# Grouped-query attention on one core: the order in which the transposed Q leaves PSUM

## The chip, the cores and the metric

The kernel runs on one core of a Trainium2 chip. The metric is the device time of one execution in microseconds; the smaller the better. A core has five engines that run their own instruction streams and meet only at semaphores: TensorE (PE: matmuls and transposes into PSUM; PEld is its loading of weights), VectorE (DVE), ScalarE (ACT), GpSimd (POOL) and SyncE (SP, which here only issues the DMAs). Inputs and outputs lie in HBM; SBUF is the working memory of 128 partitions, and PSUM takes TensorE's results.

## What is computed

Softmax attention with 32 query heads that share 8 key/value heads, for 16 sequences, 16 queries each, against 2048 keys. All inputs are bf16.

```
B, Hq, Hkv, Sq, Sk, D = 16, 32, 8, 16, 2048, 128
k = jnp.repeat(k, rep, axis=1)            # rep = Hq // Hkv = 4
v = jnp.repeat(v, rep, axis=1)
scores = jnp.einsum("bhqd,bhkd->bhqk", q, k) * D ** -0.5
p = softmax(scores, axis=-1)
return jnp.einsum("bhqk,bhkd->bhqd", p, v)
```

For each pair of a sequence and a key/value head there are 4 x 16 = 64 rows of Q, a K of 2048 x 128 and a V of 2048 x 128 (512 KB each). There are 16 x 8 = 128 such groups.

## The kernel before

**Tiling.** Two groups make a pair p, so that the 2 x 64 rows of Q fill 128 partitions; there are 64 pairs. Eight pairs share a chunk c of Q (1024 rows, `QCH`, line 19); there are 8 chunks.

**One pair** goes through these steps, each named as in the code. `K` and `V`: loads of two groups, 512 KB each. `kx` (L244, DVE, one for each group): a transpose of K in blocks of 32 x 32 words, two bf16 to a word, into `KT`. `S` (L327, PE): 32 matmuls of contraction length 32 into `S_ps`; since kx leaves the 128 values of d split into four parts, Q has to come in four matching parts x. `mx` (L251, DVE): scales the scores, copies them to `Sneg` and takes the row's extreme. `ex` (L254, ACT): exp into `P` (bf16), with the row sum. `pt` (L337, PE, two halves h): 16 transposes of P into `PT_ps`. `pe` (L274, ACT or DVE, two halves): copies `PT_ps` to `PT` in SBUF. `pv` (L342, PE): 32 matmuls of PT with V into `O_ps`. `rc` (L259, DVE): 1 / row sum. `nm` (L263 on ACT, L265 on DVE): scales and copies the result to `Osb`. `ST`: store.

**One chunk of Q** is made ready by these, each once for x = 0..3. `Q` is one load of 256 KB into `Qn`, in which partition a holds the NI = 8 rows 8a to 8a + 7. `qr` (L249; POOL, for chunk 0 DVE and ACT) picks from `Qn` the elements of part x and repeats them four times into `Qr`. `qt` (L315, PE): eight 128 x 128 transposes, one for each i, of `Qr` into `QT_ps`, one PSUM tile of 128 x 1024 bf16 whose column 128 i + a belongs to Q's row 8 a + i. `qe` (L274, ACT): copies `QT_ps` into `QT`, where column 8 a + i belongs to row 8 a + i, so that each pair's rows lie side by side for S. So qe is a copy with a change of order. There are 32 of them, and one `QT_ps`: qt of part x + 1 waits until qe of part x has read it (line 56).

**Order.** A planner in the file (`build_schedule`, lines 97 to 148) lays out a fixed order for every engine from a table of prices (`_DUR`, lines 23 to 28) and the dependencies of `make_ops` (lines 41 to 88). The engines then run these lists in order, with semaphore waits where a dependency crosses engines. In the table `("act", "qe")` stands at 1.06 us and `("act", "pe")` at 1.03. In the steady part the order of PE is S(p+1), pt(p), pv(p); of DVE mx(p), two kx, rc; of ACT ex(p), nm(p-1), pe(p, 0), pe(p, 1). Around the start of a chunk the four qr, qt and qe of the next-to-come chunk's pairs are worked in. For chunk 5 (the others from chunk 3 on are alike, eight pairs apart) the lists read:

```
ACT: ex.32 nm.31 qe.5.0 pe.32.1 qe.5.1 nm.32 qe.5.2 ex.33 qe.5.3 pe.33.0 ex.34 nm.33 pe.34.0 ex.35 nm.35 ex.36
PE:  pt.31 pv.31 qt.5.0 S.33 pt.32 qt.5.1 pv.32 qt.5.2 S.34 qt.5.3 pt.33 S.35 pv.33 pt.34 pv.34 S.36 pt.35
DVE: mx.32 kx.67 kx.68 rc.32 kx.69 pe.32.0 mx.33 kx.70 mx.34 rc.33 kx.71 pe.33.1 kx.72 mx.35 pe.34.1 rc.34 kx.73 nm.34
     rc.35 kx.74 pe.35.0 pe.35.1 mx.36
```

Chunk 0's four qt and qe come ahead of S.0; chunk 1's are spread over pairs 1 to 4.

**Loads and stores** all go through SP's queue, in the order ST(t-6), K of pair t, at times a Q, V of pair t-2. K has 10 buffers, V 14, O 8, KT and PT 3 each, Sneg and P 2 each, QT and Qn 2 each. SP waits in order, so a store that waits for its nm holds back the loads behind it.

Of the kernel before, what the change touches and what calls it, by code (L numbers as in the profile page):

```python
# [150 lines left out]
def bass_standalone__gqa_softmax__sampling_kernel(  # L151
# [14 lines left out]
    qch = min(QCH, NROWS)  # L166
    assert NROWS % qch == 0 and qch % 128 == 0
    NI = qch // 128
# [10 lines left out]
    QT = [sb(f"QT{i}", [128, 4, qch], BF16) for i in range(2)]  # L179
# [14 lines left out]
    QT_ps = ps("QT_ps", [128, 1024], BF16)  # L194
# [25 lines left out]
    def make_waiter(eng, me):  # L220
        seen = {}

        def waits(op):
            need = {}
            for d in deps[op]:
                if me == "pe" and d in where and where[d][0] == "pe":
                    continue
                s, n = wait_point(d)
                key = s.name
                if n > max(seen.get(key, 0), need.get(key, (None, 0))[1]):  # L230
                    need[key] = (s, n)
            for key, (s, n) in need.items():
                seen[key] = n
                eng.wait_ge(s, n)

        return waits

    def elementwise(eng, me):
        waits = make_waiter(eng, me)
        for op in progs[me]:  # L240
            kind, p = op[0], op[1]
            waits(op)
            if kind == "kx":
                ins = eng.transpose(KT[(p // 2) % NKT][:, p % 2, :], Kn[p % NBK][:, :])  # L244
            elif kind == "qr":
                x = op[2]
                dst = Qr[:, x, :, :].rearrange("m i (a d) -> m i a d", a=4)
                src = bass.AP(Qn[p % 2], (x // 2) * 64 + x % 2, [[NI * 128, 128], [128, NI], [0, 4], [2, 32]])
                ins = eng.activation(dst, src, ACT.Copy) if me == "act" else eng.tensor_copy(dst, src)  # L249
            elif kind == "mx":  # L250
                ins = eng.tensor_scalar(Sneg[p % 2][:, :], S_ps[:, :], -scale, None,  # L251
                                        op0=ALU.mult, op1=ALU.min, accum_out=nbias[:, p:p + 1])
            elif kind == "ex":
                ins = eng.activation(  # L254
                    P[p % 2][:, :].rearrange("m (r a j) -> m a r j", a=4, j=32),
                    Sneg[p % 2][:, :].rearrange("m (a r j) -> m a r j", a=4, j=32), ACT.Exp,
                    bias=nbias[:, p:p + 1], scale=-1.0, accum_out=rowsum[:, p:p + 1])
            elif kind == "rc":
                ins = eng.reciprocal(rrec[:, p:p + 1], rowsum[:, p:p + 1])  # L259
            elif kind == "nm":  # L260
                dst, src, r = Osb[p % NBO][:, :], O_ps[:, 0:128], rrec[:, p:p + 1]
                if me == "act":
                    ins = eng.activation(dst, src, ACT.Copy, scale=r)  # L263
                else:
                    ins = eng.tensor_scalar(dst, src, r, None, op0=ALU.mult)  # L265
            else:
                if kind == "qe":
                    dst = QT[p % 2][:, op[2], :].rearrange("d (a i) -> d i a", i=NI)
                    src = QT_ps[:, 0:qch].rearrange("d (i a) -> d i a", i=NI)
                else:  # L270
                    h = op[2]
                    dst = PT[p % NPT][:, 8 * h:8 * (h + 1), :]
                    src = PT_ps[h][:, :].rearrange("k (t m) -> k t m", t=8)
                ins = eng.activation(dst, src, ACT.Copy) if me == "act" else eng.tensor_copy(dst, src)  # L274
            ins.then_inc(sem_eng[me], 1)

    with nc.Block() as block:  # L277

        @block.gpsimd
        def _(gp):  # L280
            gp.iota(iota_t[:, :], [[1, 128]], base=0, channel_multiplier=-1).then_inc(sem_id, 1)
            gp.wait_ge(sem_id, 1)
            gp.tensor_scalar(ident[:, :], iota_t[:, :], 0.0, None, op0=ALU.is_equal).then_inc(sem_id, 1)
            elementwise(gp, "pool")
# [65 lines left out]
        @block.vector  # L350
        def _(dve):
            elementwise(dve, "dve")

        @block.scalar
        def _(act):
            elementwise(act, "act")
# [28 lines left out]
```

## Time and profile before

| | |
|---|---|
| median of 3 runs | 478.08 us (477.15 to 480.02) |
| the profiled execution's own time | 474.86 us |
| its span, from the first to the last instruction | 473.1 us |
| PE busy | 275.6 us (58%) |
| mean granted clock of TensorE | 0.825 of full speed |
| bytes read from HBM / written | 136.31 MB / 2.10 MB |

The span in 40 slices of 11.8 us: each digit is the busy share of an engine in tenths (9 is 90% or more), PEclk the clock that was granted to TensorE in tenths, and the last line what the DMA engines moved.

```profile
PE   1147547737655566646666456654666645675754
PEld 1115435525443354433544234442544424454543
DVE  5237567936795478955799366993579645889994
ACT  6859987999499966999588993899948799479894
POOL 0200000300003000110003000030000300000000
PEclk9999877975898677966899667995579776779999
DMA  8951978995889549995599839998299972999990
GB/s 300 413 220 49 348 265 286 360 413 182 308 315 401 197 169 407 352 361 182 213 406 400 319 133 332 340 408 306 89 353 320 401 278 115 340 337 363 411 367 10
```

A digit 3 of POOL marks the four qr of a chunk, so the chunks can be counted from that line. In a list of groups, a row has the line, the engine and its operation, output and input by name and shape, the count, then busy time and mean duration in ns, then the engine's idle time ahead of such instructions and what ended it. Matmuls overlap in the array, so their durations don't add up to PE's time.

### The profile page before, as it was taken

Reading aid. Unit: us, or ns where it says so; the run is one execution under the profiler, and the core shown is the slowest. Engines: PE = TensorE matmul, PEld = TensorE weight load, DVE = VectorE, ACT = ScalarE, POOL = GpSimd, SP = SyncE. Lnnn points to the kernel's source line nnn. Section 1 sums busy time; section 2 is a strip of 40 time slices with the busy share of each in tenths; the row PEclk is TensorE's granted clock in tenths of the full one; section 3 lists DMA queues with packets and bytes.
Section 4 is the critical chain, followed back from the end, with each engine's and each line's share of the span. In section 5 each row is a group of like instructions: output and inputs, shape, how many; then the busy total and the mean of one; then the engine's idle time right before and its main releaser. Section 6 shows DMA issues by size and latency. Waiting matters only on the chain.

```text
span 473.1 us, 11999 instructions
## 1 busy us (share of the span) xinstructions
PE 275.6 (58%) x5376; PEld 194.3 (41%) x5376; DVE 327.2 (69%) x369; ACT 381.1 (81%) x308; POOL 28.9 (6%) x34
## 2 busy tenths in 40 slices
PE   1147547737655566646666456654666645675754
PEld 1115435525443354433544234442544424454543
DVE  5237567936795478955799366993579645889994
ACT  6859987999499966999588993899948799479894
POOL 0200000300003000110003000030000300000000
PEclk9999877975898677966899667995579776779999
DMA  8951978995889549995599839998299972999990
GB/s 300 413 220 49 348 265 286 360 413 182 308 315 401 197 169 407 352 361 182 213 406 400 319 133 332 340 408 306 89 353 320 401 278 115 340 337 363 411 367 10
DMA packets 47282, 139.19 MB, mean 294 GB/s; under 512 B 13440, under 2 KB 13440, under 8 KB 47232
## 3 DMA queue, kind: packets, MB, share of 16 engines
q1 hardware_dynamic: 47232, 138.43, 77.9%
q8 instruction: 42, 0.69, 0.6%
q14 instruction: 8, 0.07, 0.0%
HBM read 136.31 MB, written 2.10 MB: 293 GB/s over the span
## 4 chain that ended last, share of the span: by engine, by line
issue 16%; ACT 14%; PE 12%; DVE 4%; DMA 3%; POOL 1%; SPq 1%; ACTq 0%; POOLq 0%
ACT PT L274 7%; ACT QT L274 5%; PE S_ps L327 4%; PE O_ps L342 4%; PE PT_ps L337 3%; DMA Qn<-in_q_dram 3%; ACT P L254 2%; DVE Sneg L251 1%; DVE PT L274 1%; POOL Qr L249 1%; DVE KT L244 1%; PE QT_ps L315 1%; SPq L301 1%; ACTq L277 0%; ACT O L263 0%
## 5 line engine op out<-in xcount | busy, mean ns | idle before, releaser
L251 DVE TENSOR_SCALAR_CACHE_REDUCE Sneg<-S_ps 128x2048 f32<-128x2048 f32 x64 | 146.5, 2289 | 66.2 <-PE S_ps L327 64.1
L274 ACT ACTIVATE QT<-QT_ps 128x1024 bf16<-128x1024 bf16 x32 | 151.1, 4723 | 13.5 <-PE QT_ps L315 13.4
L244 DVE STREAM_TRANSPOSE KT<-Kn 128x1024 int32<-128x1024 int32 x128 | 153.5, 1225 | 2.4 <-DMA Kn<-in_k_dram 2.3
L254 ACT ACTIVATE P<-Sneg,nbias 128x2048 bf16<-128x2048 f32 x64 | 129.3, 2020 | 8.8 <-DVE Sneg L251 8.6
L342 PE MATMUL O_ps<-Vb,PT 128*64 128x128 bf16 x2048 | 82.6, 243 | 77.1 <-ACT PT L274 69.8
L274 ACT ACTIVATE PT<-PT_ps 128x1024 bf16<-128x1024 bf16 x92 | 94.9, 1072 | 31.2 <-PE PT_ps L337 31.2
L342 PEld LDWEIGHTS O_ps<-Vb,PT 128*64 128x64 bf16 x2048 | 71.2, 125 | 92.6 <-ACT PT L274 81.9
L327 PE MATMUL S_ps<-KT,QT 32*64 32x512 bf16 x2048 | 89.5, 469 | 21.3 <-DVE KT L244 13.7
L337 PE MATMUL PT_ps<-ident,P 128*128 128x128 bf16 x1024 | 84.4, 248 | 11.8 <-ACT P L254 11.6
L337 PEld LDWEIGHTS PT_ps<-ident,P 128*128 128x128 bf16 x1024 | 72.2, 113 | 40.5 <-ACT P L254 29.0
L315 PE MATMUL QT_ps<-ident,Qr 128*128 128x128 bf16 x256 | 27.0, 270 | 84.6 <-ACT QT L274 56.7
L315 PEld LDWEIGHTS QT_ps<-ident,Qr 128*128 128x128 bf16 x256 | 20.4, 120 | 93.0 <-issue 77.6
L327 PEld LDWEIGHTS S_ps<-KT,QT 32*64 32x64 bf16 x2048 | 30.7, 120 | 49.8 <-issue 20.7
L249 POOL COPY Qr<-Qn 128x1024 bf16<-128x1024 bf16 x28 | 28.0, 1040 | 347.9 <-DMA Qn<-in_q_dram 346.7
L274 DVE COPY PT<-PT_ps 128x1024 bf16<-128x1024 bf16 x36 | 24.1, 689 | 32.1 <-PE PT_ps L337 32.0
L263 ACT ACTIVATE O<-O_ps,rrec 128x128 bf16<-128x128 f32 x53 | 20.9, 394 | 30.6 <-PE O_ps L342 30.3
L259 DVE RECIPROCAL rrec<-rowsum 128x1 f32<-128x1 f32 x64 | 9.1, 143 | 24.7 <-ACT P L254 24.6
L265 DVE TENSOR_SCALAR O<-O_ps,rrec 128x128 bf16<-128x128 f32 x11 | 3.9, 351 | 14.8 <-PE O_ps L342 14.8
L254 ACT ACTIVATION_READ_ACCUMULATOR P<-Sneg,nbias 128x1 f32 x64 | 12.5, 195 | 0.0
L251 DVE DVE_READ_ACCUMULATOR Sneg<-S_ps 128x1 f32 x64 | 5.3, 83 | 0.0
L249 DVE COPY Qr<-Qn 128x1024 bf16<-128x1024 bf16 x2 | 1.3, 690 | 3.4 <-DMA Qn<-in_q_dram 3.4
L249 ACT ACTIVATE Qr<-Qn 128x1024 bf16<-128x1024 bf16 x2 | 2.0, 1050 | 1.4 <-DMA Qn<-in_q_dram 1.4
(7 smaller groups left out, 2.5 us busy)
## 6 DMA issues: line engine op xcount, KB each, us to landing
Kn<-in_k_dram SPq DMA_DIRECT2D x128, 512.0 KB, 6.4
Vb<-in_v_dram SPq DMA_DIRECT2D x128, 512.0 KB, 8.0
Qn<-in_q_dram SPq DMA_DIRECT2D x8, 256.0 KB, 6.1
out_dram<-O SPq DMA_DIRECT2D x64, 32.0 KB, 4.7
```

Source lines behind the costliest of these rows:

```text
L244: ins = eng.transpose(KT[(p // 2) % NKT][:, p % 2, :], Kn[p % NBK][:, :])
L249: ins = eng.activation(dst, src, ACT.Copy) if me == "act" else eng.tensor_copy(dst, src)
L251: ins = eng.tensor_scalar(Sneg[p % 2][:, :], S_ps[:, :], -scale, None, op0=ALU.mult, op1=ALU.min, accum_out=nbias[:, p:p + 1])
L254: ins = eng.activation(P[p % 2][:, :].rearrange("m (r a j) -> m a r j", a=4, j=32), Sneg[p % 2][:, :].rearrange("m (a r j) -> m a r j", a= ...
L259: ins = eng.reciprocal(rrec[:, p:p + 1], rowsum[:, p:p + 1])
L263: ins = eng.activation(dst, src, ACT.Copy, scale=r)
L274: ins = eng.activation(dst, src, ACT.Copy) if me == "act" else eng.tensor_copy(dst, src)
L301: sp.dma_start(dst, src).then_inc(sem_dma[kind][s], 16)
L315: ins = pe.transpose(QT_ps[:, 128 * i:128 * (i + 1)], Qr[:, x, i, :], ident[:, :],)
L327: ins = pe.matmul(S_ps[64 * gg:64 * (gg + 1), 512 * a:512 * (a + 1)], QT[c % 2][32 * a:32 * (a + 1), x, 128 * pp + 64 * gg:128 * pp + 64 * ...
L337: ins = pe.transpose(PT_ps[h][:, 128 * t:128 * (t + 1)], P[p % 2][:, 128 * r:128 * (r + 1)], ident[:, :])
L342: ins = pe.matmul(O_ps[64 * gg:64 * (gg + 1), 0:128], PT[p % NPT][:, r, 64 * gg:64 * (gg + 1)], Vb[(2 * p + gg) % NBV][:, r, :], start=(r ...
```

## The change

In qe the loop order of the copy is turned round. Before, the copy walks `QT_ps` in its own order (i outside, a inside), reads 1024 columns in one run, and writes each at column 8 a + i of `QT`: consecutive writes are 8 elements (16 bytes) apart. After, it walks `QT` in its own order (a outside, i inside), writes 1024 columns in one run, and reads column 128 i + a of `QT_ps`: consecutive reads are 128 elements (256 bytes) apart, eight of them for each a. Every element goes from the same place to the same place as before. Nothing else in the kernel is touched.

```
             else:
                 if kind == "qe":
-                    dst = QT[p % 2][:, op[2], :].rearrange("d (a i) -> d i a", i=NI)
-                    src = QT_ps[:, 0:qch].rearrange("d (i a) -> d i a", i=NI)
+                    dst = QT[p % 2][:, op[2], :].rearrange("d (a i) -> d a i", i=NI)
+                    src = QT_ps[:, 0:qch].rearrange("d (i a) -> d a i", i=NI)
                 else:
                     h = op[2]
```

## The prediction

> **What bounds the kernel now.** I read the page's shares first, then its groups, then the order of time around one hand-over to a new Q chunk, then waits, chain and windows. From the page:
>
> ```profile
> span 473.1 us, 11999 instructions
> ...
> PE 275.6 (58%) x5376; PEld 194.3 (41%) x5376; DVE 327.2 (69%) x369; ACT 381.1 (81%) x308; POOL 28.9 (6%) x34
> ...
> q1 hardware_dynamic: 47232, 138.43, 77.9%
> ...
> L274 ACT ACTIVATE QT<-QT_ps 128x1024 bf16<-128x1024 bf16 x32 | 151.1, 4723 | 13.5 <-PE QT_ps L315 13.4
> ...
> L254 ACT ACTIVATE P<-Sneg,nbias 128x2048 bf16<-128x2048 f32 x64 | 129.3, 2020 | 8.8 <-DVE Sneg L251 8.6
> L274 ACT ACTIVATE PT<-PT_ps 128x1024 bf16<-128x1024 bf16 x92 | 94.9, 1072 | 31.2 <-PE PT_ps L337 31.2
> ...
> L249 ACT ACTIVATE Qr<-Qn 128x1024 bf16<-128x1024 bf16 x2 | 2.0, 1050 | 1.4 <-DMA Qn<-in_q_dram 1.4
> ...
> out_dram<-O SPq DMA_DIRECT2D x64, 32.0 KB, 4.7
> ```
>
> ACT is the fullest engine, and its largest group is the one that the change touches. The two L274 rows are copies of the same size by the same engine from PSUM to SBUF: PT takes 1.07 us, QT 4.72 us. They differ in the order of the elements: QT's write steps 16 bytes between 2-byte elements. But 81% is a mean over two stages. The order of time around the start of one chunk (qe.5, pairs 32 to 36) parts them; the columns are start, duration, engine, line, operation, and in brackets the idle time before it:
>
> ```profile
> 239.13 2.29 DVE L251 TENSOR_SCALAR_CACHE_REDUCE Sneg<-S_ps 128x2048 f32<-128x2048 f32 x1
> ...
> 253.36 2.29 DVE L251 TENSOR_SCALAR_CACHE_REDUCE Sneg<-S_ps 128x2048 f32<-128x2048 f32 x1
> ...
> 255.58 2.37 DVE L244 STREAM_TRANSPOSE KT<-Kn 128x1024 int32<-128x1024 int32 x2
> 255.70 2.00 ACT L254 ACTIVATE P<-Sneg,nbias 128x2048 bf16<-128x2048 f32 x1
> ...
> 255.87 1.08 PE L342 MATMUL O_ps<-Vb,PT 128*64 128x128 bf16 x32 [1.58 <-ACT PT L274]
> ...
> 258.02 1.08 PE L327 MATMUL S_ps<-KT,QT 32*64 32x512 bf16 x32
> ...
> 258.12 4.76 ACT L274 ACTIVATE QT<-QT_ps 128x1024 bf16<-128x1024 bf16 x1
> ...
> 259.03 1.07 PE L337 MATMUL PT_ps<-ident,P 128*128 128x128 bf16 x16
> 259.69 0.69 DVE L274 COPY PT<-PT_ps 128x1024 bf16<-128x1024 bf16 x1 [0.55 <-PE PT_ps L337]
> ...
> 263.02 0.66 PE L315 MATMUL QT_ps<-ident,Qr 128*128 128x128 bf16 x8 [2.93 <-ACT QT L274]
> ...
> 263.83 1.92 PE L342 MATMUL O_ps<-Vb,PT 128*64 128x128 bf16 x32
> ...
> 269.52 1.93 PE L327 MATMUL S_ps<-KT,QT 32*64 32x512 bf16 x32
> ...
> 271.52 2.29 DVE L251 TENSOR_SCALAR_CACHE_REDUCE Sneg<-S_ps 128x2048 f32<-128x2048 f32 x1 [7.78 <-PE S_ps L327]
> ...
> 276.19 1.89 PE L337 MATMUL PT_ps<-ident,P 128*128 128x128 bf16 x16 [0.69 <-ACT P L254]
> ...
> 292.12 2.28 DVE L251 TENSOR_SCALAR_CACHE_REDUCE Sneg<-S_ps 128x2048 f32<-128x2048 f32 x1
> ```
>
> From mx.29 (239.13) to mx.32 (253.36) three pairs take 14.23 us, 4.74 a pair: the dense stage. From mx.32 to mx.36 (292.12) four pairs take 38.76 us, 9.7 a pair: the hand-over. PE executes in order: qt.5.1 (263.02) waits for QT_ps, which ACT is still emptying, S.34 (269.52) stands behind qt.5.2, and DVE idles 7.78 us for S.34. The wait list says it for the whole span (total us, times, longest):
>
> ```profile
> DVE Sneg L251 <- PE S_ps L327: 64.1, 14, 15.6
> PE QT_ps L315 <- ACT QT L274: 56.7, 18, 4.9
> ```
>
> The chain that ended last shows mx.36 and mx.52, two chunks of eight pairs later: 116.9 us, so 58.5 a chunk.
>
> ```profile
> 292.21 2.21 DVE Sneg L251 x2
> ...
> 409.11 2.21 DVE Sneg L251 x2
> ```
>
> What binds the dense stage, and what DMA can do, the windows show (stretch, busy us of PE, PEld, DVE, ACT, POOL, then granted clock, DMA share, GB/s):
>
> ```profile
> 8.00:28.00 20.00, 3.06 (x24) 2.33 (x24) 6.23 (x5) 16.45 (x4) 4.04 (x4) 1.00 1.03 412
> ...
> 232.00:263.00 31.00, 18.04 (x448) 12.76 (x433) 30.05 (x34) 24.04 (x25) 3.99 (x4) 1.00 1.03 404
> ...
> 430.00:460.00 30.00, 19.51 (x495) 14.17 (x492) 29.64 (x31) 26.47 (x32) 0.00 (x0) 1.00 1.01 398
> ```
>
> In the dense windows DVE is busy 30.05 of 31.00 us and the DMA engines are full at about 400 GB/s. So the hand-over is bound by ACT's QT copies, the dense stage by DVE, with DMA at its heels.
>
> **The change, part by part.** It removes and adds no instruction, wait, semaphore or DMA. The planner's prices are untouched, so every engine's order (SP's queue too) stays; line 27 prices qe at 1.06 us, so the order is one laid out for a copy of that length. Only the 32 QT copies change: the write becomes one run of 2048 bytes, and the read takes 128 runs of eight elements that lie 256 bytes apart in PSUM.
>
> Price of the new copy. No row of the trace reads PSUM at a step. Low end: 1.05 us, the Qr row, where ACT reads SBUF at a 4-byte step and pays nothing for it. High end: 4.72 us, if jumps in a read cost what they cost in a write; more than that is not excluded (rival 3). I take 1.07 us: after the edit the copy has the PT row's engine, size, types, memories and write, and differs from it in the order of the read alone. The P row, whose write hops between 64-byte runs at 0.99 ns an element, shows that a jump now and then is not dear.
>
> [...]
>
> At 1.07 us each copy is 3.65 us shorter, in all 32 x 3.65 = 116.8 us of ACT. What of it lies on the path:
>
> (a) Start. The first QT copy starts at 5.64, the sixth transpose of K ends at 14.56, and S.0 starts at 28.11:
>
> ```profile
> 5.64 4.70 ACT L274 ACTIVATE QT<-QT_ps 128x1024 bf16<-128x1024 bf16 x1 [0.24 <-PE QT_ps L315]
> ...
> 8.21 6.35 DVE L244 STREAM_TRANSPOSE KT<-Kn 128x1024 int32<-128x1024 int32 x5 [1.96 <-DMA Kn<-in_k_dram]
> ```
>
> ```profile
> 28.11 1.93 PE L327 MATMUL S_ps<-KT,QT 32*64 32x512 bf16 x32 [4.88 <-ACT QT L274]
> ```
>
> Between stand only four transposes and four copies by turns, so S.0 starts 4 x 3.65 = 14.6 us sooner, at 13.5, and ends at 15.4, when DVE is free (14.56). Nothing of this is covered.
>
> (b) Six hand-overs, qe.2 to qe.7. Walked with the durations above, from the first mx at 0: ex 2.3 to 4.3, then nm, qe.0 to 5.8, ACT's PT copy (pt ends 6.7) to 7.8, qe.1 to 8.9, nm, qe.2 9.6 to 10.7, ex of the second pair to 12.8, qe.3 to 13.9, PT copy to 15.0, ex of the third pair to 17.1. On PE, qt.2 runs right behind pv at 9.0, and S of the third pair starts at 9.6. On DVE the third mx starts at 10.8, the fourth at 16.3 behind two kx and a PT copy, the fifth at 23.8 behind two kx, an nm and three PT copies. So 23.8 us for four pairs instead of 38.8: 15.0 saved, six times, 90 us. DVE is busy for some 22 of the 23.8; what is late next is DVE itself and no longer S.
>
> (c) The hand-over of chunk 1, spread over pairs 1 to 4, has the same four copies: 14.6 us on ACT. DVE would still need some 6 us a pair, so I count 12.
>
> Sum: 14.6 + 90 + 12 = 117, all of ACT's gain; 473.1 - 117 = 356. From the other side, DVE's work is 327.2 us; with 7 idle before mx.0, some 2 us of stall in each of seven hand-overs, and 10 at the end, 358.
>
> Then the cover: SP issues loads behind stores that wait for nm, so earlier nm means earlier loads, and DMA becomes the other bound. The first windows show the slow start:
>
> ```profile
> 0.00:5.00 5.00, 0.40 (x5) 0.43 (x6) 1.29 (x2) 2.89 (x3) 0.97 (x6) 1.00 0.59 190
> 5.00:10.00 5.00, 0.61 (x6) 0.34 (x4) 3.03 (x3) 4.76 (x2) 0.00 (x0) 1.00 0.95 369
> ...
> 270.00:275.00 5.00, 1.97 (x38) 0.88 (x23) 2.30 (x2) 5.00 (x2) 0.00 (x0) 0.50 0.98 348
> ```
>
> 138.43 MB at 412 to 398 GB/s take 336 to 348 us; the first ten us move 2.8 MB, which is 3 us lost; and K.127 lands six V loads (3.1 MB, 7.8 us) before V.127, while it has kx, S, mx, ex, pt, two PT copies, pv, nm and a store (4.7) ahead, some 15 us with waits, so the end lies 6 to 9 us behind the last V. Together 345 to 360. A chunk thus needs 17.3 MB / 0.400 = 43.3 us of DMA and 23.8 + 4 x 4.74 = 42.8 of DVE and ACT. Two bounds of one height will wait for each other at times: I add 4 to 358, a choice that no row measures. Span 362.
>
> The profiled execution took 474.86 us, 1.8 over its span, and the median of the runs is 478.08, 3.2 more. 362 + 1.8 + 3.2 = **367 us**.
>
> **The rivals.**
>
> 1. The read pays what the write paid. For it: the only row with a large step is dear. Against it: that row is a write of half-words, and no row shows a slow read. The copy stays at 4.7 us and the time at 478, within 0.5%. [...] Chance 0.05.
> 2. The read goes at half pace: 2 x 0.99 ns x 1024 = 2.0 us, 0.95 over the forecast, DVE's slack taking a tenth: 367 + 32 x 0.95 x 0.9 = 394 us. For and against as in 1. Chance 0.08.
> 3. Slower: PSUM's read is dearer than SBUF's write. Its place is the same copy; it decides from 4.72 us up, and each further us costs 32, since (a) to (c) put all of it on the path: at 6 us, 478 + 41 = 519. For it: 256 bytes is a longer step than 16. Against it: ACT's other groups read PSUM (PT) or hop (P, Qr), and none but the stepped write is slow. Chance 0.04.
> 4. The copy is short, but TensorE's granted clock stays low in the hand-overs. The window at 270 was granted 0.50, and there S takes 1.93 us against 1.08, pt 1.89 against 1.07, pv 1.92 against 1.08: 2.5 us more a pair, about half of it on the path. In 28 hand-over pairs that is 35 us, 402 at worst, and 385 if half of them are cold. Against it: the dense window at 232 was granted 1.00 with PE idle 13 of 31 us, and the stretch at 270 comes behind waits of PE for ACT (2.93 us at 263.02), which go. Chance 0.07.
>
> That the edit doesn't do what it says can be left out: both forms bring element (i, a) of QT_ps to place 8a + i of QT.
>
> **How the numbers follow.** Forecast 0.76; rivals 0.05, 0.08, 0.04 and 0.07. The forecast's own range is 354 (nothing lost where the bounds meet, DMA at 412) to 382 (DMA at 398 and 15 us lost there). With the half-cold case it reaches to 388; left out are rivals 1 to 3 and the worst of 4, 0.2 together. So 354 to 388. Faster by over 0.5% (about what a measurement of this kernel can tell from no change): 0.76 + 0.08 + 0.07 = 0.91; within 0.5%: 0.05; slower: 0.04.
>
> **What the new profile would show.** The QT row of L274 near 1.07 us, ACT busy near 265 us; S.0 near 13.5; hand-overs near 24 us for four pairs, without a wait of DVE for S_ps over 2 us in them; DMA share over 0.95 in nearly all of the span, and DVE busy for about 90% of it. The prediction is wrong at its first step if the QT row is over 1.3 us. It is wrong in its sum if the row is short but DVE still waits long for S (order or clock), or if waits of L244 for Kn pass some 15 us (DMA under 398 GB/s).

## The result, and the profile after

The changed kernel took 373.31 us (median of 4 runs, 367.76 to 375.11) against 478.79 us before (477.15 to 480.02): 0.772 of the time, 95% interval 0.764 to 0.781. Two of the four runs (374.96 and 375.11) count as slow, being over 1.5% above the fastest, and the ratios here and below compare fast runs alone. The forecast was 367 us, the range 354 to 388. In two later comparisons the same kernel gave 371.88 and 369.66 us; the 12 runs together lie between 366.75 and 376.26, median 371.6. The profiled execution took 371.66 us, with a span of 369.9.

The page of the changed kernel: shares, slices, the queue, and the groups that answer to those shown of before.

```profile
span 369.9 us, 11999 instructions
## 1 busy us (share of the span) xinstructions
PE 250.0 (68%) x5376; PEld 177.2 (48%) x5376; DVE 325.7 (88%) x369; ACT 268.0 (72%) x308; POOL 28.9 (8%) x34
...
DVE  4889899999749888999698999979989989799993
ACT  5387778966649477894587957869388865788883
...
PEclk9999699997878869998598998989879987899999
DMA  7999999999999799999999999999999999999960
GB/s 266 416 408 410 410 409 410 410 411 411 411 411 348 264 413 361 395 415 404 400 360 402 400 375 381 382 414 385 379 406 361 409 362 408 400 376 411 410 241 9
...
q1 hardware_dynamic: 47232, 138.43, 96.1%
...
L274 ACT ACTIVATE PT<-PT_ps 128x1024 bf16<-128x1024 bf16 x92 | 90.2, 1021 | 46.0 <-PE PT_ps L337 46.0
...
L274 ACT ACTIVATE QT<-QT_ps 128x1024 bf16<-128x1024 bf16 x32 | 32.6, 1020 | 9.8 <-PE QT_ps L315 9.8
```

The QT row fell from 4723 to 1020 ns and is now the PT row to a nanosecond: ACT's read of PSUM at a 256-byte step costs nothing here. ACT lost 113 us of work (381.1 to 268.0); PE's and DVE's instructions are the same. DVE has become the fullest engine at 88%, and the DMA engines are busy for 96% of the span instead of 78%, at 410 GB/s in long stretches. Two things in the slices are not as they should be: at slices 13 and 14 (about 110 to 130 us) the rate drops to 348 and 264 GB/s, and the granted clock still has digits of 5 and 6.

The wait list after (total us, times, longest):

```profile
PE O_ps L342 <- ACT PT L274: 57.6, 40, 1.6
...
DVE Sneg L251 <- PE S_ps L327: 16.6, 18, 1.7
...
PE QT_ps L315 <- POOL Qr L249: 5.3, 4, 3.2
...
PE QT_ps L315 <- ACT QT L274: 3.8, 4, 1.2
```

DVE's wait for S fell from 64.1 to 16.6 us, its longest from 15.6 to 1.7; PE's wait for the QT copies from 56.7 to 3.8. PE's wait for qr, that is for Q's load, was there before with 4.5 us in four waits, the longest 2.2; now its longest is 3.2.

### The profile page after: what moved, and what is told of

Same layout as the page of the kernel before. It is cut to its first block, busy times and chain, and to the rows that moved or that the text cites. A ratio compares the mean times of both kernels' runs of the same rounds, so it can differ in the third digit from the quotient of the medians.

```text
span 369.9 us, 11999 instructions
## 1 busy us (share of the span) xinstructions
PE 250.0 (68%) x5376; PEld 177.2 (48%) x5376; DVE 325.7 (88%) x369; ACT 268.0 (72%) x308; POOL 28.9 (8%) x34
## 3 DMA queue, kind: packets, MB, share of 16 engines
q1 hardware_dynamic: 47232, 138.43, 96.1%
## 5 line engine op out<-in xcount | busy, mean ns | idle before, releaser
L251 DVE TENSOR_SCALAR_CACHE_REDUCE Sneg<-S_ps 128x2048 f32<-128x2048 f32 x64 | 146.3, 2287 | 18.5 <-PE S_ps L327 16.6
L342 PE MATMUL O_ps<-Vb,PT 128*64 128x128 bf16 x2048 | 76.0, 232 | 71.9 <-ACT PT L274 57.6
L274 ACT ACTIVATE PT<-PT_ps 128x1024 bf16<-128x1024 bf16 x92 | 90.2, 1021 | 46.0 <-PE PT_ps L337 46.0
L342 PEld LDWEIGHTS O_ps<-Vb,PT 128*64 128x64 bf16 x2048 | 65.4, 117 | 86.0 <-ACT PT L274 65.3
L327 PE MATMUL S_ps<-KT,QT 32*64 32x512 bf16 x2048 | 83.1, 437 | 22.9 <-DVE KT L244 18.7
L337 PEld LDWEIGHTS PT_ps<-ident,P 128*128 128x128 bf16 x1024 | 65.4, 106 | 36.4 <-ACT P L254 25.1
L337 PE MATMUL PT_ps<-ident,P 128*128 128x128 bf16 x1024 | 77.2, 235 | 7.9 <-ACT P L254 7.5
L327 PEld LDWEIGHTS S_ps<-KT,QT 32*64 32x64 bf16 x2048 | 29.4, 113 | 48.1 <-DVE KT L244 24.5
L274 ACT ACTIVATE QT<-QT_ps 128x1024 bf16<-128x1024 bf16 x32 | 32.6, 1020 | 9.8 <-PE QT_ps L315 9.8
L263 ACT ACTIVATE O<-O_ps,rrec 128x128 bf16<-128x128 f32 x53 | 19.3, 364 | 28.2 <-PE O_ps L342 27.9
L274 DVE COPY PT<-PT_ps 128x1024 bf16<-128x1024 bf16 x36 | 23.8, 680 | 11.6 <-PE PT_ps L337 11.3
L315 PE MATMUL QT_ps<-ident,Qr 128*128 128x128 bf16 x256 | 22.7, 240 | 14.5 <-POOL Qr L249 5.3
L315 PEld LDWEIGHTS QT_ps<-ident,Qr 128*128 128x128 bf16 x256 | 17.3, 107 | 19.3 <-issue 8.4
L251 DVE DVE_READ_ACCUMULATOR Sneg<-S_ps 128x1 f32 x64 | 5.3, 83 | 0.0
```

What stands on the lines that cost most here:

```text
L315: ins = pe.transpose(QT_ps[:, 128 * i:128 * (i + 1)], Qr[:, x, i, :], ident[:, :],)
L327: ins = pe.matmul(S_ps[64 * gg:64 * (gg + 1), 512 * a:512 * (a + 1)], QT[c % 2][32 * a:32 * (a + 1), x, 128 * pp + 64 * gg:128 * pp + 64 * ...
L337: ins = pe.transpose(PT_ps[h][:, 128 * t:128 * (t + 1)], P[p % 2][:, 128 * r:128 * (r + 1)], ident[:, :])
L342: ins = pe.matmul(O_ps[64 * gg:64 * (gg + 1), 0:128], PT[p % NPT][:, r, 64 * gg:64 * (gg + 1)], Vb[(2 * p + gg) % NBV][:, r, :], start=(r ...
```

## The experiments

**Where the time of a chunk lies.** The 64 `mx` rows (DVE, L251) in order of time give the pace; mx.8c to mx.8c+4 is a hand-over of four pairs, mx.8c+4 to mx.8c+8 the four dense pairs behind it. Means over chunks 3 to 7 (the pairs 16 to 55), worked out from these starts in each profile; `clock` is the mean granted clock of TensorE in the five stretches of dense pairs, the last column the median time of the runs (for the changed kernel's first row that of all its 12):

```
kernel                           hand-over   dense   clock   chunk   span    median
before                              38.6      19.6    0.93    58.2   473.1   478.8
the prediction's walk               23.8      19.0            42.8
changed                             24.7      20.8    0.84    45.4   369.9   371.6
changed, the two later profiles     25.9      20.7    0.85    46.7   374.4   371.9
                                    24.5      20.9    0.84    45.4   369.8   369.7
changed, QT copies made twice       26.0      20.7    0.85    46.7   381.9   383.3
changed, every other copy slow      33.4      18.8    1.00    52.3   428.0   428.0
changed, Q's loads a pair earlier   22.5      21.9    0.77    44.5   361.5   362.8
changed, transposes added           25.7      19.4    0.93    45.1   366.1   367.1
changed, both of these              22.8      19.8    0.91    42.6   356.6   358.2
changed, half of V loaded           22.8      21.1    0.83    43.9   362.5   365.3
```

So the walk of the hand-over was 0.9 us short and the dense pairs 1.8: together 2.6 us a chunk and 13 us in these five chunks, about the 12 that separate the span from the walk's 358. Of the 1.8 us, 0.6 were there before the change: the walk took its 4.74 us a pair from a stretch with a granted clock of 1.00, and the five stretches before have 19.6 us for four pairs. In all rows the dense pairs are the slower the lower their clock, from 18.8 us at 1.00 to 21.9 at 0.77. Three profiles of the one changed kernel differ by 1.4 us in the hand-over and by 0.2 in the dense pairs, so a difference of 1 us in a hand-over shows little.

**1. The price of the copy by its step.** Behind the last pair, copies of one 128 x 1024 tile are made one at a time, each on its own line, with the step of the read or the write varied:

```
+            act.activation(y2(b_, 8), y1(q_, 8), ACT.Copy) ...      # read PSUM at 256 bytes
...
+            act.activation(x1(b_, 2), x2(q_, 2), ACT.Copy) ...      # write bf16 at 4 bytes
...
```

> After the last pair, copies of one 128 x 1024 tile are made one at a time into tiles that nobody reads, each on a line of its own, with the step of the read or the write varied; the answer is the duration of each. [...]

From the order of time behind the last pair (start, us, engine, line; the table has all copies); `q_` is QT_ps, `scb` and `scs` are bf16 tiles in SBUF, `scf` is float32:

```profile
359.91 1.02 ACT L374 ACTIVATE scb<-QT_ps 128x1024 bf16<-128x1024 bf16 x1
...
360.97 1.02 ACT L376 ACTIVATE scb<-QT_ps 128x1024 bf16<-128x1024 bf16 x1
...
362.02 1.02 ACT L378 ACTIVATE scb<-QT_ps 128x1024 bf16<-128x1024 bf16 x1
363.08 1.30 ACT L380 ACTIVATE scb<-QT_ps 128x1024 bf16<-128x1024 bf16 x1
...
364.42 2.43 ACT L382 ACTIVATE scb<-QT_ps 128x1024 bf16<-128x1024 bf16 x1
366.88 4.69 ACT L384 ACTIVATE scb<-QT_ps 128x1024 bf16<-128x1024 bf16 x1
...
380.71 1.02 ACT L390 ACTIVATE scf<-QT_ps 128x1024 f32<-128x1024 bf16 x1
381.77 1.07 ACT L392 ACTIVATE scf<-QT_ps 128x1024 f32<-128x1024 bf16 x1
382.87 1.96 ACT L394 ACTIVATE scf<-QT_ps 128x1024 f32<-128x1024 bf16 x1
...
386.89 1.06 ACT L398 ACTIVATE scb<-scs 128x1024 bf16<-128x1024 bf16 x1
...
389.93 2.00 ACT L402 ACTIVATE scb<-scs 128x1024 bf16<-128x1024 bf16 x1
391.97 0.69 DVE L358 COPY scd<-QT_ps 128x1024 bf16<-128x1024 bf16 x1 [28.20 <-ACT scb L402]
392.70 1.23 DVE L360 COPY scd<-QT_ps 128x1024 bf16<-128x1024 bf16 x1
393.96 4.68 DVE L362 COPY scd<-QT_ps 128x1024 bf16<-128x1024 bf16 x1
```

By line, in us, one copy each:

| what steps | one run | 4 B | 8 B | 16 B | 32 B | 64 B | 256 B |
|---|---|---|---|---|---|---|---|
| ACT, read of PSUM (L374, L378, L376) | 1.02 | | | 1.02 | | | 1.02 |
| ACT, write of bf16 to SBUF (L374, L380 to L388) | 1.02 | 1.30 | 2.43 | 4.69 | 4.44 | 4.61 | |
| ACT, write of float32 to SBUF (L390 to L396) | 1.02 | | 1.07 | 1.96 | 2.00 | | |
| ACT, read of bf16 from SBUF (L398 to L402) | 1.06 | | | 2.00 | | | 1.92 |
| DVE, read of PSUM (L358, L360) | 0.69 | | | | | | 1.23 |
| DVE, write of bf16 to SBUF (L358, L362) | 0.69 | | | 4.68 | | | |

The price of a bf16 write depends on its step: ACT's grows from 1.02 us in one run to 1.30, 2.43 and 4.69 at 4, 8 and 16 bytes, and goes no higher at 32 and 64 (4.44 and 4.61). At 16 bytes that is 4.6 ns for each of the 1024 elements. A float32 write takes 1.07 us at 8 bytes and 1.96 at 16, and a bf16 read of SBUF 2.00 at 16, so these two cost 1.9 and 2.0 ns an element at that step. ACT's read of PSUM costs nothing at the steps tried: 1.02 us at 16 and 256 bytes, as in one run. No run shows what lies behind these prices; why a bf16 write is dearer than a float32 one was not tried.

**2. The price of ACT's time: each copy twice.**

```
+                if kind == "qe":
...
+                    eng.activation(scq[:, :], src, ACT.Copy).then_inc(sem_dup, 1)
                 ins = eng.activation(dst, src, ACT.Copy) ...
```

> Each of the 32 QT copies is made twice, the first time into a tile that nobody reads, so ACT spends 2.04 us in place of 1.02 at that place. Theory A (what counts is ACT's time in the hand-over, and nearly all of it lies on the path, as the prediction's rival 2 prices it): 32 x 1.02 x 0.9 = +29 us, 398 to 404. Theory B (the changed kernel is bound by DVE and the transfers, ACT has 28% of slack): +10 us or less, 375 to 383.

383.32 us, ratio to before 0.805 (0.798 to 0.811), against 371.88 of the changed kernel on the same chip: 11.4 us for 32.6 us of added work, 0.35 of it. That is between the two theories and at the edge of B. The mean hand-over grew by 1.4 us for 4.1 us of copies, and this mean hides two changes that go against each other. The hand-over of chunk 3, for which Q lands late in the changed kernel (experiment 4), fell from 28.6 to 24.9 us, and PE's longest wait for qr from 3.2 to 1.0. The other four grew from 23.7 to 26.3 us in the mean, by 2.6 us or 0.64 of the added work; against the hand-overs of experiment 4's kernel, where PE waits for qr only 0.8 us in all (22.5), it is 3.5 us or 0.86. These are single profiles, but 0.35 is a net figure and not the price of ACT's time where Q is there. The windows of two hand-overs of the changed kernel (chunks 4 and 5), with the dense pairs between them, show what fills them (stretch, busy us of PE, PEld, DVE, ACT, POOL, granted clock, DMA share, GB/s):

```profile
149.21:171.55 22.34, 15.79 (x368) 11.60 (x366) 21.89 (x26) 17.71 (x21) 3.99 (x4) 1.00 1.03 407
171.55:193.28 21.73, 14.97 (x307) 10.06 (x308) 18.74 (x22) 15.08 (x18) 0.00 (x0) 0.76 1.01 384
193.28:217.50 24.22, 17.33 (x368) 12.32 (x366) 21.92 (x27) 17.80 (x21) 3.99 (x4) 0.93 1.01 389
```

In the first hand-over DVE is busy for 21.89 of 22.34 us and ACT has 4.6 us to spare; in the next DVE is busy for as long, but the hand-over takes 24.22. ACT's spare time doesn't take up the second copies whole: PE's wait for the QT copies grew from 3.8 us in 4 waits to 21.4 in 20, since the copies and transposes go through the single QT_ps by turns. The second row, the four dense pairs, is taken up in experiment 5.

**3. Half of the change undone.**

```
+                    if op[2] % 2:
+                        dst = QT[p % 2][:, op[2], :].rearrange("d (a i) -> d i a", i=NI)
+                        src = QT_ps[:, 0:qch].rearrange("d (i a) -> d i a", i=NI)
```

> The copies of parts x = 1 and 3 write at the 16-byte step again, those of 0 and 2 stay as changed. Theory A (each copy's 3.7 us lies on the path by itself): 16 x 3.7 = +59 us, 425 to 437, the two kinds at 4.7 and 1.02 us in one profile. Theory B (two slow copies of a hand-over hide behind DVE): +35 us or less, under 408.

428.01 us (423.08 to 430.27), ratio 0.891 (0.882 to 0.899): by the medians 56 us over the changed kernel, by the ratios (0.778 for the changed kernel beside it) 54, for 59.2 us of added ACT time (the 32 copies take 91.8 us in all and not 32.6). Theory A's forecast holds here, and B's does not. The hand-over grew by 8.8 us for 7.4 us of ACT, and the dense pairs became 1.9 us shorter, at a granted clock of 1.00 in all five stretches. So of this larger addition nearly the whole lies on the path. The price of ACT's time is not one number: 0.35 net in experiment 2, some 0.9 here. How much of the difference is ACT's spare time, how much Q's landing and how much the clock, these two runs do not part.

**4. What the changed kernel loses: Q that lands late.** The order of time of the changed kernel where the rate dropped:

```profile
94.63 1.50 SPq L301 DMA_DIRECT2D Qn<-in_q_dram  x1
...
99.76 2.29 DVE L251 TENSOR_SCALAR_CACHE_REDUCE Sneg<-S_ps 128x2048 f32<-128x2048 f32 x1
...
105.44 3.99 POOL L249 COPY Qr<-Qn 128x1024 bf16<-128x1024 bf16 x4 [39.37 <-DMA Qn<-in_q_dram]
...
106.53 1.03 PE L315 MATMUL QT_ps<-ident,Qr 128*128 128x128 bf16 x8 [3.17 <-POOL Qr L249]
...
110.43 0.69 DVE L274 COPY PT<-PT_ps 128x1024 bf16<-128x1024 bf16 x1 [4.89 <-PE PT_ps L337]
...
111.04 2.28 DVE L251 TENSOR_SCALAR_CACHE_REDUCE Sneg<-S_ps 128x2048 f32<-128x2048 f32 x1
```

The load of Q for chunk 3 is issued at 94.63 into a full queue (a DMA share of 1.03 and 410 GB/s from 85 to 105 us) and lands at 105.4, 10.8 us later (the median of such loads was 6.1 us before and is 6.3 now). PE waits for qr with pt queued behind qt, DVE stands for 4.89 us, and mx.17 starts 11.3 us after mx.16. Then the stores are late and hold back the loads behind them (between 100 and 135 us SP waited five times for ACT's nm, 20.7 us in all), and the DMA rate drops in the next slices. Before the change the rate fell to 49 to 182 GB/s in one slice of each hand-over, so the queue was not full all the time. The three profiles of the changed kernel have 5.3, 8.6 and 12.4 us of PE's waits for qr. The experiment moves the loads of Q for chunks 2 to 7 one pair ahead in SP's list:

```
+    sp_l = progs["sp"]
+    for c in range(2, n_qch):
+        i = sp_l.index(("Q", c))
+        sp_l.insert(i - 5, sp_l.pop(i))
```

> The loads of Q for chunks 2 to 7 stand one pair earlier in SP's queue; all else as changed. Theory Q (a part of the loss over the walk is Q that lands late behind a full DMA queue: PE waited 3.2 us for qr at 103 to 106 us and then ran cold): the hand-over of chunk 3 falls from 28.6 to about 24 us, waits of PE for qr vanish, 364 to 370. Theory N (Q's landing only moves the wait): 369 to 375.

362.84 us (362.64 to 363.31), ratio 0.759 (0.756 to 0.763). From its wait list:

```profile
PE QT_ps L319 <- POOL Qr L253: 0.8, 1, 0.8
```

The hand-over of chunk 3 took 23.1 us instead of 28.6, all five 22.3 to 23.1. Theory Q holds. The four runs lie within 0.7 us, where the twelve of the changed kernel lie 9.5 apart; that Q's landing made this spread is likely, but not shown. The gain is smaller than the hand-overs alone would give: the dense pairs behind them took 21.9 us instead of 20.8, at a granted clock of 0.77 in all five stretches. Of the 8.3 us by which the span is shorter, some 5 lie in the five chunks of the table and some 4 in the first 16 pairs.

**5. The granted clock behind a hand-over.** In the changed kernel, behind the hand-over of chunk 3 (pairs 21 and 22):

```profile
133.04 1.89 PE L337 MATMUL PT_ps<-ident,P 128*128 128x128 bf16 x16
133.16 2.29 DVE L251 TENSOR_SCALAR_CACHE_REDUCE Sneg<-S_ps 128x2048 f32<-128x2048 f32 x1
...
136.10 1.92 PE L342 MATMUL O_ps<-Vb,PT 128*64 128x128 bf16 x32 [1.18 <-ACT PT L274]
...
137.95 1.85 PE L327 MATMUL S_ps<-KT,QT 32*64 32x512 bf16 x32
...
139.88 2.29 DVE L251 TENSOR_SCALAR_CACHE_REDUCE Sneg<-S_ps 128x2048 f32<-128x2048 f32 x1 [1.65 <-PE S_ps L327]
...
144.54 2.29 DVE L251 TENSOR_SCALAR_CACHE_REDUCE Sneg<-S_ps 128x2048 f32<-128x2048 f32 x1
```

pt, pv and S take 1.89, 1.92 and 1.85 us instead of 1.07, 1.08 and 1.08, DVE waits 1.65 us for S, and this pair takes 6.7 us; the next takes 4.66. The granted clock from 133.04 to 139.88 was 0.52. A chunk later the second window row above has 0.76 for its four dense pairs, in which PE is busy for 14.97 us; three such stretches of the kernel before, at a clock of 1.00, have 11.5 to 11.8. To tell cause from sign, PE is given work that nothing uses, where it waits for ACT:

```
+                if kind == "pt" and op[2] == 1 and p % 8 in (2, 3, 4, 5, 6) and 16 <= p < 56:
+                    pe.wait_ge(sem_eng["act"], where[("qe", p // 8 + 1, 3)][1])
+                    for i in range(12):
+                        pe.transpose(QT_ps[:, 128 * (i % 8):128 * (i % 8 + 1)], ident[:, :], ident[:, :])
```

> Twelve transposes of the identity into the idle QT_ps are added after pt in 28 pairs behind hand-overs (pairs 2 to 6 of chunks 2 to 6 and 18 to 22 alike), in stretches where PE waits for ACT. They compute nothing that is used. Theory C (the dense pairs behind a hand-over run at 5.2 us and not at 4.74 because TensorE's granted clock falls to half there): granted clock over 0.95, pairs back at 4.74, 8 to 12 us less, 360 to 365. Theory D (those pairs wait for something else, the clock is a sign of it): the clock rises and the time stays at 369 to 375, or grows by the added work.

The added work is 300 transposes, in 25 pairs (the expectation's 28 was a miscount); its row, and PE's wait for qr:

```profile
L352 PE MATMUL QT_ps<-ident 128*128 128x128 bf16 x300 | 22.2, 227 | 0.0
```

```profile
PE QT_ps L315 <- POOL Qr L249: 8.8, 5, 4.0
```

367.06 us (364.70 to 368.71), ratio 0.768 (0.763 to 0.773). The mean granted clock rose from 0.906 to 0.938 (0.906 to 0.919 in the three profiles of the changed kernel), not over 0.95, and the dense pairs fell from 20.8 to 19.4 us for four, clear of the 20.7 to 20.9 of those three. The hand-overs, 25.7 us, and PE's wait for qr, 8.8 us, lie within what the unchanged orders show (24.5 to 25.9 us, and 5.3, 8.6 and 12.4). Theory C's mechanism holds; its 8 to 12 us were some 4 (371.6 to 367.1), where the dense pairs alone would give 6.7 in five chunks. What took the rest, these runs do not show; the next experiment does the same with Q in time.

**6. Both together, and the transfers.**

> Q's loads one pair earlier and the twelve added transposes in 28 pairs, both. Theory C (late Q and the low clock are two losses that add up): the dense pairs come to 4.8 to 5.0 us, as with the transposes alone, the hand-overs stay at 22 to 24, 353 to 359. Theory T (with Q in time the transfers are the next bound, at 17.3 MB a chunk): hand-overs or dense pairs wait for K or Q again, 360 to 364, the same as with the earlier Q alone.

358.20 us (357.31 to 359.29), ratio 0.748 (0.743 to 0.753): 4.6 us under the earlier Q alone, with no run of the one among those of the other, and the dense pairs fell from 21.9 to 19.8. So the two losses add up. A chunk takes 42.6 us where the walk had 42.8, the span 356.6 where it had 358. The agreement is partly luck: the hand-over is 1.0 us shorter than the walk's, the dense pairs, at 0.91 of the clock, 0.8 longer. That span was reached with 138.43 MB, so the transfers were not what kept the changed kernel from the walk, other than through Q.

With 30 MB less to load:

> From the fifteenth group on, only the first half of each V tile is loaded, the rest of the buffer keeps what was there; 30 MB less are moved, the output is not the reference's. Theory T (the transfers cost what the kernel loses over DVE's walk): 358 to 362, DMA share near 0.75. Theory D (DVE's and PE's order binds): 368 to 374, as before.

365.33 us (362.22 to 366.72), ratio 0.764 (0.759 to 0.769): between the two, and close to that of the earlier Q. With less in the queue Q lands sooner: the qr of chunk 3 start at 100.15 us and not at 105.44, and PE waited once for qr, 1.0 us. The hand-overs are those of the earlier Q (22.8 against 22.5 us) and the time is no better than there (362.84), so Q's landing is enough to explain this gain, and the run shows no other cost of the transfers.

With the copies of PT on ACT alone:

> The planner may give the copies of PT to ACT alone, so DVE loses 36 copies (24 us) and ACT gains 37 us; the orders are laid out anew. Theory V (DVE's load binds the changed kernel): 355 to 362. Theory T (the transfers bind, or ACT becomes the chain): 368 to 380.

358.41 us (357.04 to 361.56), ratio 0.751 (0.746 to 0.756), in the range of Theory V. But this run changes more than DVE's load: all orders are new, and the granted clock of the dense pairs was 1.00 in all five stretches. So it agrees with a load of DVE that binds, and does not show it. PE still waited 20.6 us for qr. With the earlier Q besides:

> Q's loads one pair earlier and the copies of PT on ACT alone. Theory V (DVE's load and late Q are two losses): 350 to 355. Theory T (138.43 MB at 412 GB/s, 336 us, with the start and the end make 345 to 350 the floor, and the kernel with PT on ACT alone is there already, DMA share 0.98): 355 to 359.

357.64 us (357.22 to 359.42), ratio 0.748 (0.742 to 0.753), no faster. In its wait list the next bound appears:

```profile
DVE KT L248 <- DMA Kn<-in_k_dram: 23.7, 41, 1.8
```

DVE waits for K 41 times, 23.7 us in all, against 1.9 us in one wait in the changed kernel, and PE 17.6 us for V: here the transfers bind. So the earlier Q with the transposes, or PT's copies on ACT with or without the earlier Q, gives some 358 us, 12 us better than the changed kernel on the same chip (369.66) and 25% under the kernel before.

The changed kernel beside these runs, for reference:

> The changed kernel once more, beside the runs below on the same chip. Both theories: 366 to 376 us, QT copies at 1.02 us.

> The changed kernel a third time, as the reference of the two runs below on the same chip: 367 to 376 us.

371.88 us (369.37 to 376.26) and 369.66 us (366.75 to 372.18).

## Why the prediction was right

- **The price of the copy**: 1.07 us forecast, 1.02 measured. The choice of the PT row as the nearest was right, and rival 1 (the read pays what the write paid) and rival 3 (more than that) fell: the probe has PSUM reads by ACT at 1.02 us at 16 and at 256 bytes. That the step of the write was the whole cost is shown by 4.69 us in the probe.
- **The start**: S.0 was forecast at 13.5 and began at 13.38.
- **The hand-overs**: 23.8 us forecast, 24.7 measured in the mean. Without chunk 3's late Q the other four have 22.3 to 24.8, and 22.5 with the earlier Q. That DVE and no longer S would be late next was right in the best of them, 21.89 of 22.34 us busy; in the next DVE's 21.92 us stand in 24.22.
- **The sum** (a) to (c): 14.6, 90 and 12 us forecast; mx.0 came 14.7 us sooner, the six hand-overs together were 81 us shorter, the first eight pairs 13. The dense pairs behind the hand-overs, which the sum left as they were, took back 5. So 103 us came off the span and not 117.
- **The term that was mis-sized** is the one called a choice: 4 us for two bounds of one height that wait for each other. The walk alone gave 358, the span was 369.9, so it was 12. Two things made it up: Q, which the prediction took to be in time, though PE waited 4.5 us for qr before, and for which PE now waited up to 3.2 us at a stretch, and four dense pairs that cost 20.8 us and not 19.0 at a granted clock of 0.84. With most of both taken away a chunk takes 42.6 us against the walk's 42.8.
- **Rival 4** had the right mechanism in the wrong place. The low clock was priced for the hand-overs. The argument against it, that PE's waits go, held there: the granted clock in the five hand-overs was 0.65 to 0.77 before and 0.82 to 1.00 after. It did not hold for the dense pairs behind them, which had 0.84 to 1.00 before and 0.76 to 0.91 after.
- **Rival 2's price** was wrong: it laid 0.9 of ACT's added time on the path. With two copies of 1.02 us in place of one of 2.04 it was 0.35 net, so a read at half pace would have given about 383 and not 394 us. The forecast took the slope of the kernel before for the one after.
- **The range's lower end**, 354, does not follow from the terms given for it: the walk's 358 with nothing lost where the bounds meet, and the offsets of 1.8 and 3.2, make 363.
- **The offset** of 3.2 us from the profiled execution to the median was 1.65 for the changed kernel (371.66 to 373.31). So the forecast of the span was 7.9 us too low, and 1.6 of that was made up for by chance.

## What to carry to other kernels

Where ACT copies 2-byte elements from PSUM to SBUF in another order, let the read take the step and write in one run: ACT's read of PSUM cost nothing here at the two steps tried (1.02 us at 16 and 256 bytes, as in one run), and a step of 16 bytes on the write cost 3.7 us a tile (4.69 us). When a copy that was the bound gets short, look for what now meets a full queue: a small load in the same list of DMAs, issued just in time, came late (PE waited 4.5 us for it in all before, 5.3 to 12.4 after), and moving it one pair ahead was worth 9 us. The price of an engine's time is no constant: 32.6 us more of ACT cost 11.4 net, 59.2 us cost some 55, and the mean of the hand-overs hid that Q's lateness went away as the copies grew. And when one stage gets faster, look at the granted clock of the stage behind it, where the loss may turn up again: here it fell from 0.93 to 0.84 in the dense pairs, and four of them took 20.8 us instead of 19.6.

## What was not expected of the hardware

A bf16 write to SBUF grows with its step, 1.02, 1.30, 2.43 and 4.69 us for 1024 elements in one run and at 4, 8 and 16 bytes, and then stays (4.44 and 4.61 us at 32 and 64 bytes), on ACT and DVE alike at 16 bytes (4.69 and 4.68 us). A float32 write and a bf16 read of SBUF at 16 bytes cost 1.96 and 2.00 us. DVE does pay for a read of PSUM at 256 bytes, 1.23 against 0.69 us; ACT does not. And the low granted clock moved from the hand-overs to the dense pairs as the hand-overs got shorter; its means were 0.71 and 0.93 before, 0.92 and 0.84 after, 1.00 and 0.77 with the earlier Q. There 300 transposes that compute nothing, 22 us of PE in all, brought the dense pairs back to 0.91 and the time from 362.84 to 358.20 us.
